# An attention and feed-forward kernel: one projection moved from block 2 to the end of block 1, and eight more filler matmuls in the opening

## Chip, cores, metric

One core of one Trainium2 chip. The metric is the device time of an execution in microseconds. Each run also has a profile, whose span (first to last instruction) is some 1.8 us shorter than the time of the same execution. TensorE is called PE, VectorE DVE, ScalarE ACT, GpSimd POOL, SyncE SP.

## The reference, cut to what matters

For each of 8 batches and 8 heads, K and V (1024 x 64) are projected along the sequence by E and F to 64 rows; q attends to these; the result, 8192 x 512, goes through a feed-forward layer with a quick GELU.

```python
k_proj = np.einsum('ks,bhsd->bhkd', E, k)
v_proj = np.einsum('ks,bhsd->bhkd', F, v)
scores = scale * np.matmul(q, k_proj.transpose(0, 1, 3, 2))
...                                   # softmax over the 64
x = np.matmul(attn, v_proj)           # to (8192, 512)
h = x @ w_in                          # 512 -> 2048
out = (h * (1.0 / (1.0 + np.exp(-1.702 * h)))) @ w_out
```

## The kernel before

It works in 16 blocks of 512 tokens, two to a batch. A block has 16 groups of four matmuls (ffn1, slots 0 to 15), then eight of eight (ffn2, slots O to O+7, with O = 16). Attention of later blocks is put into these slots: `at(j, slot, ...)` says behind which part of block j a piece comes. Each engine is given its work in the order of the program: in the profile DVE casts k_b of batch 2 at 100.95 us, behind the norm(3, 0) that stands ahead of it, though PE had ended that projection at 95.7. In norm(h, u) and scores(h, u), h counts blocks of 512 tokens (two to a batch) and u halves of the heads, so scores(4, 0) is the first attention of batch 2. The PSUM pools of the program have eight buffers in all, called banks here: four for f_ps, two for d_ps, two for n_ps.

```python
ps_f = ctx.enter_context(tc.tile_pool(name="ps_f", bufs=4, space=PSUM))
ps_d = ctx.enter_context(tc.tile_pool(name="ps_d", bufs=2, space=PSUM))
ps_n = ctx.enter_context(tc.tile_pool(name="ps_n", bufs=2, space=PSUM))

def load(b):                          # issued by POOL at the start of block 2(b-2)
    load_kv(k, kt, b, "k_sb")         # one buffer: waits for the projection of b-1
    if b == 1:
        load_kv(v, vt, b, "v_sb")
    load_q(b)                         # eight DMAs
    if b > 1:
        load_kv(v, vt, b, "v_sb")

def warm(n):                          # fillers: PE works on zeros, meant to keep its clock up
    w_ps = f_tile([P, TB])
    for _ in range(n):
        nc.tensor.matmul(w_ps, zeros[:, :P], zeros, start=True, stop=True)

def proj(b):                          # 16 matmuls, K and V in turn
    def go():
        kvps[b] = f_tile([P, H, D])
        for j in range(J):
            for e, r in enumerate((LO, HI)):
                nc.tensor.matmul(kvps[b][r], eft(j, slice(e * KP, (e + 1) * KP)),
                                 (kt, vt)[e][b][:, :, j, :], start=(j == 0), stop=(j == J - 1))
    return go

def kv_out(b):                        # DVE casts k_b, SP transposes it by DMA, DVE copies V
    ...
        nc.vector.tensor_copy(k_b, ps[LO])
        if b > 1:
            nc.sync.dma_start_transpose(out=kts[b % 2], in_=k_b.rearrange("k h d -> k (h d)"))
        v_out(b, ps)
...
at(1, O + 4, q_dma(2))                # SP transposes q of batch 2 by DMA
at(2, 1, norm(3, 0))                  # two reciprocals and two products on DVE
at(2, 2, proj(2), kv_out(2))
at(2, 11, norm(3, 1))
at(2, O, ...scores(4, 0)...)          # the first that needs kts of batch 2
```

The opening (the calls ahead of block 0) does the attention of the first tokens while K, Q, V, w_in and w_out arrive on one queue of POOL, in that order (later parts of Q come between V and w_in and among w_in); fillers stand where PE would wait.

The softmax here doesn't subtract the row's maximum and nothing guards it: scores larger than these inputs give would overflow.

## Time and profile before

| | |
|---|---|
| time, median of the 6 runs beside the change | 514.50 us (513.2 to 515.5) |
| execution that was profiled | 516.17 us, span 514.4 us, mean granted clock 0.996 |
| PE busy in that profile | 499.3 us |
| first K matmul, first ffn1, first ffn2 | 10.01, 23.46, 40.47 us |
| projection of batch 1, of batch 2, scores(4, 0) | 66.56, 93.81, 110.44 us |

### The profile page before, as it was taken

To read this page: it belongs to the slowest core of one execution; us is meant where nothing else is said; L and a number is where in the kernel's file an instruction comes from. 1 tells how busy PE (TensorE), PEld (TensorE's weight loads), DVE (VectorE), ACT (ScalarE), POOL (GpSimd) and SP (SyncE) were. 2 spreads that over 40 slices of the span, in tenths; PEclk is the share of its full clock that TensorE was granted. 3 is DMA by queue.
4 is the path that set the end of the run, shared out by engine and by line. 5 is a ranking of instruction groups with operands and counts; after the bars stand their busy time and mean duration, and the time that the engine had idled before them with its cause. 6 is when DMAs were issued, how large, how long until landed. Compare 5 with 4: busy or idle time off the path is not lost.

```text
span 514.4 us, 7185 instructions
## 1 busy us (share of the span) xinstructions
PE 499.3 (97%) x3040; PEld 232.0 (45%) x3090; DVE 171.6 (33%) x222; ACT 264.8 (51%) x444; POOL 78.0 (15%) x97
## 2 busy tenths in 40 slices
PE   6999999999999999999999999999999999999997
PEld 3585444434444444444444444444444444444444
DVE  4432214763871521416242251615214161511000
ACT  1576454554637446373655627375473737244351
POOL 6542051512400051000510023000000000000000
PEclk9999999999999999999999999999999999999999
DMA  9999999999999089670996339990602305050102
GB/s 157 197 202 207 190 152 171 214 157 134 210 118 240 1 142 215 129 178 6 223 179 181 76 80 217 121 246 1 169 1 59 107 3 163 1 165 1 82 1 82
DMA packets 124200, 66.58 MB, mean 129 GB/s; under 512 B 92252, under 2 KB 116060, under 8 KB 122248
## 3 DMA queue, kind: packets, MB, share of 16 engines
q0 software_dynamic: 84400, 29.37, 51.8%
q1 hardware_dynamic: 39688, 36.49, 28.2%
q8 instruction: 24, 0.39, 0.3%
q10 hardware_dynamic: 80, 0.26, 0.2%
q14 instruction: 8, 0.07, 0.0%
HBM read 70.78 MB, written 16.96 MB: 171 GB/s over the span
## 4 chain that ended last, share of the span: by engine, by line
PE 91%; DMA 3%; DVE 2%; issue 2%; ACT 1%; DVEq 0%; POOLq 0%
PE f_ps L401 42%; PE f_ps L369 40%; PE f_ps L166 2%; PE f_ps L263 2%; DMA kt<-k_b 2%; DMA k_sb<-in_k_dram 2%; DVE rdn L318 1%; PE n_ps L263 1%; PE f_ps L174 1%; PE n_ps L355 1%; PE d_ps L340 1%; PE d_ps L298 0%; PE f_ps L136 0%; PE f_ps L393 0%; DVE xT L319 0%
## 5 line engine op out<-in xcount | busy, mean ns | idle before, releaser
L369 PE MATMUL f_ps<-xT,w_in_sb 128*128 128x512 bf16 (+1 forms) x1071 | 225.4, 366 | 0.9
L401 PE MATMUL f_ps<-w_out_sb,gT 128*128 128x512 bf16 x976 | 221.5, 379 | 4.0 <-issue 3.5
L372 ACT ACTIVATE gT<-f_ps 128x512 bf16<-128x512 f32 (+1 forms) x270 | 152.1, 573 | 62.9 <-PE f_ps L369 61.7
L369 PEld LDWEIGHTS <-w_in_sb 128*128 128x128 bf16 x1088 | 105.5, 98 | 115.6 <-issue 2.1
L401 PEld LDWEIGHTS <-gT 128*128 128x128 bf16 x1008 | 95.5, 98 | 120.2 <-issue 11.3
L404 ACT COPY o_sb<-f_ps 128x512 f32<-128x512 f32 x63 | 36.9, 586 | 130.8 <-PE f_ps L401 121.0
L328 DVE TENSOR_TENSOR xT<-n_ps,rbc 128x512 bf16<-128x512 f32 x44 | 28.4, 686 | 203.3 <-PE n_ps L263 123.8
L301 DVE RECIPROCAL rden<-d_ps 128x512 f32<-128x512 f32 x22 | 72.2, 3322 | 0.0
L64 POOL DMA_DIRECT2D q_sb<-in_q_dram x56 | 49.1, 901 | 54.1 <-DMA k_sb<-in_k_dram 42.5
L279 ACT ACTIVATE expT<-f_ps 128x512 bf16<-128x512 f32 (+1 forms) x68 | 35.1, 571 | 27.8 <-PE f_ps L263 27.8
L58 POOL DMA_DIRECT2D k_sb<-in_k_dram x10 | 8.4, 845 | 175.6 <-PE f_ps L166 159.2
L318 DVE RECIPROCAL rdn<-d_ps 128x512 f32<-128x512 f32 x8 | 26.8, 3353 | 6.5 <-PE d_ps L263 6.5
L279 ACT ACT_TABLE_LOAD x13 | 16.7, 1283 | 5.8 <-PE f_ps L263 5.6
L220 DVE CAST k_b<-f_ps 64x512 bf16<-64x512 f32 x7 | 4.8, 682 | 44.2 <-PE f_ps L166 44.2
L283 ACT ACT_TABLE_LOAD x14 | 18.0, 1283 | 0.2
L166 PE MATMUL f_ps<-k_sb,eft 128*64 128x512 bf16 x56 | 13.4, 382 | 0.0
L166 PE MATMUL f_ps<-v_sb,eft 128*64 128x512 bf16 x56 | 13.4, 382 | 0.0
L395 DVE COPY o_sb<-f_ps 128x256 f32<-128x256 f32 x1 | 0.4, 425 | 38.6 <-issue 38.6
L263 PE MATMUL f_ps<-qT,kt 64*32 64x512 bf16 x240 | 12.3, 387 | 1.0 <-DMA kt<-k_b 1.0
L136 PE MATMUL f_ps<-zeros 128*128 128x512 bf16 x25 | 9.3, 484 | 1.6 <-DVE zeros L107 1.2
L263 PEld LDWEIGHTS <-kt 64*32 64x32 bf16 x272 | 4.0, 89 | 14.5 <-issue 12.9
L263 PE MATMUL n_ps<-expT,vq 64*32 64x512 bf16 x208 | 10.4, 377 | 0.0
(71 smaller groups left out, 132.7 us busy)
## 6 DMA issues: line engine op xcount, KB each, us to landing
out_dram<-o_sb SPq DMA_DIRECT2D x15, 1024.0 KB
rbc<-rdr SPq DMA_DIRECT2D x22, 512.0 KB
k_sb<-in_k_dram POOLq DMA_DIRECT2D x7, 1024.0 KB, 14.1
v_sb<-in_v_dram POOLq DMA_DIRECT2D x7, 1024.0 KB, 10.4
q_sb<-in_q_dram POOLq DMA_DIRECT2D x56, 128.0 KB, 14.0
w_in_sb<-in_moe_w_in_dram POOLq DMA_DIRECT2D x8, 256.0 KB, 11.7
w_out_sb<-in_moe_w_out_dram POOLq DMA_DIRECT2D x4, 512.0 KB, 14.8
out_dram<-o_sb SPq DMA_DIRECT2D x3, 256.0 KB
```

Of the source, the lines that this page charges most:

```text
L64: nc.gpsimd.dma_start(out=qt[b][:, j], in_=qv[:, j])
L166: nc.tensor.matmul(kvps[b][r], eft(j, slice(e * KP, (e + 1) * KP)), (kt, vt)[e][b][:, :, j, :], start=(j == 0), stop=(j == J - 1))
L263: nc.tensor.matmul(outs[i][r.start + c:r.start + c + 32], lhsTs[i][ri, c:c + 32], rhss[i][ri], start=True, stop=True)
L279: nc.scalar.activation(expT[h][:, 2 * u + i, ts], s_ps[i], AF.Exp, scale=scale)
L283: nc.scalar.preload_act_table(AF.Gelu_apprx_sigmoid)
L301: nc.vector.reciprocal(rden[:, e, :], d_ps[e])
L318: nc.vector.reciprocal(rd, d_ps[i])
L328: nc.vector.tensor_tensor(x_of(h)[:, 2 * u + i, :], n_ps[i], rbc[h][:, 2 * u + i, :], op=ALU.mult)
L369: nc.tensor.matmul(h_ps, w_in_sb[:, kc, fc * P:(fc + 1) * P], xT[j][:, kc, ts], start=(kc == 0), stop=(kc == KC - 1))
L372: nc.scalar.activation(gts[j][:, fc, ts], h_ps, AF.Gelu_apprx_sigmoid)
L401: nc.tensor.matmul(o_ps[n], gts[j][:, fc, n * P:(n + 1) * P], w_out_sb[:, fc, :], start=(fc == 0), stop=(fc == FC - 1))
L404: nc.scalar.copy(osb[j][:, n, :], o_ps.pop(n))
```

## The change

The intent: batch 2 gets projected before norm(3, 0) loads DVE, so that the transposed k_b is there when scores(4, 0) asks; and the fillers of the opening leave the four f_ps banks and fill more of the gaps, so that the clock of PE stays up.

```diff
--- before.py
+++ after.py
@@ -131,7 +131,7 @@
         return ps_f.tile(shape, dt, name="f_ps")
 
     def warm(n):
-        w_ps = f_tile([P, TB])
+        w_ps = ps_n.tile([P, TB], F32, name="n_ps")
         for _ in range(n):
             nc.tensor.matmul(w_ps, zeros[:, :P], zeros, start=True, stop=True)
 
@@ -150,7 +150,7 @@
     for i in range(2):
         nc.vector.tensor_copy(ffs[:, i * J // 2:(i + 1) * J // 2],
                               efts[i][:, :, None, KP:].to_broadcast([P, J // 2, 2, KP]))
-    warm(2)
+    warm(4)
 
     def eft(j, cols=slice(0, 2 * KP)):
         return efts[j // (J // 2)][:, j % (J // 2), cols]
@@ -179,7 +179,7 @@
         k_ps = proj0(0, h0, n)
         k_b = att.tile([KP, n, D], BF16, name=f"k0_b{h0}", bufs=1)
         nc.vector.tensor_copy(k_b, k_ps[LO])
-        warm(1)
+        warm(2)
         k_tr(0, k_b, h0 // 2)
 
     def k_tr(b, k_b, p0):
@@ -422,14 +422,15 @@
     warm(2)
     for u in range(2):
         scores(0, u, 0)()
+    warm(4)
+    v_piece(0, 4)
     warm(3)
-    v_piece(0, 4)
-    warm(2)
     for p in range(2):
         tok(0, p, 0)()
     v_piece(4, 2)
     warm(1)
     x_tr(0, 0, 0)()
+    warm(1)
     tok(0, 2, 0)()
     x_tr(0, 1, 0)()
     v_piece(6, 2)
@@ -471,7 +472,7 @@
         at(j, O + 5, gelu_table)
     at(1, O + 4, q_dma(2))
     at(2, 1, norm(3, 0))
-    at(2, 2, proj(2), kv_out(2))
+    at(1, O + 7, proj(2), kv_out(2))
     at(2, 11, norm(3, 1))
     at(2, O + 6, proj(3), kv_out(3), norm(4, 0))
     at(2, O, q_dma(3))
```

## The prediction

> **What bounds the kernel now.** I read the page first. Part 1 says that TensorE is busy for nearly the whole span, and part 2 that it runs at full clock in every slice:
>
> ```profile
> PE 499.3 (97%) x3040; PEld 232.0 (45%) x3090; DVE 171.6 (33%) x222; ACT 264.8 (51%) x444; POOL 78.0 (15%) x97
> PEclk9999999999999999999999999999999999999999
> ```
>
> So only idle time or slow clock of TensorE can be saved: 514.4 less 499.3 is 15.1 us of idle. The second view is the list of waits of PE alone, from 28 us to the end. It has two lines:
>
> ```profile
> PE f_ps L401 <- issue: 3.5, 22, 0.2
> PE f_ps L263 <- DMA kt<-k_b: 1.0, 1, 1.0
> ```
>
> The reader is to see that after 28 us one single wait is worth naming, 1.0 us, once. All else that a schedule can save lies in the first 28 us (15.1 less 4.5 makes 10.6 us of idle there, most of it before the first data arrive). The change goes for these two places.
>
> The third view is the chain that ended last, near that wait (start, length, what):
>
> ```profile
> 92.74 3.37 DVE rdn L318
> 96.20 0.69 DVE xT L319
> 96.89 3.27 DVE rdn L318
> 100.26 0.69 DVE xT L319
> 100.95 0.59 DVE k_b L220
> 101.57 8.82 DMA kt<-k_b
> 110.44 0.41 PE f_ps L263 x8
> ```
>
> Batch 2 is projected at 93.8 to 95.7, but VectorE takes the queue of two reciprocals and two products of norm(3, 0) first (8.1 us), casts k_b at 100.95, and the DMA transpose lands 8.82 us later, 1.0 us after PE wanted scores(4, 0).
>
> The fourth view is the timeline, of POOL and of PE, for what the earlier place of the projection needs:
>
> ```profile
> 80.98 0.87 POOL L58 DMA_DIRECT2D v_sb<-in_v_dram  x1 [0.33 <-issue]
> ...
> 88.74 1.89 PE L401 MATMUL f_ps<-w_out_sb,gT 128*128 128x512 bf16 x8
> 90.47 1.89 PE L369 MATMUL f_ps<-xT,w_in_sb 128*128 128x512 bf16 x8
> ```
>
> and the DMA view of 80 to 96 us:
>
> ```profile
> v_sb<-in_v_dram POOLq DMA_DIRECT2D x1, 1024.0 KB, 10.6
> ```
>
> V of batch 2 is issued at 80.98 and lands 10.6 us later, at 91.6. The new place of the projection is reached by PE at 90.6, when the last part of block 1 ends (the first row of block 2 starts at 90.47, and the chain has it take over at 90.63).
>
> The fifth view is busy time and clock in the opening, in stretches that I chose by the clock (PE, PEld, DVE, ACT, POOL, then PEclk, DMA share, GB/s):
>
> ```profile
> 11.67:15.08 3.41, 3.41 (x26) 2.12 (x27) 1.03 (x5) 0.00 (x0) 1.98 (x3) 0.51 1.31 204
> 8.26:11.67 3.41, 1.36 (x11) 0.92 (x11) 0.56 (x2) 0.00 (x0) 1.00 (x2) 0.99 1.42 195
> 4.85:8.26 3.41, 2.00 (x14) 0.85 (x12) 1.75 (x6) 1.20 (x2) 3.24 (x5) 1.00 1.15 156
> ```
>
> PE runs at half clock from 11.67 to 15.08, after a stretch in which it was busy for 1.36 of 3.41 us; the stretch before, with 2.00 of 3.41, was followed by full clock.
>
> [...] one half-speed stretch of 3.41 us, and one filler takes 0.63 us in it and 0.38 us outside. [...] these stretches put it between 40% and 59%, if the records' busy time is what counts. [...] The rows around the 1.0 us wait show no other matmul slipping in. [...] The program's pools take 4, 2 and 2, so the fillers get no new bank: they move from f_ps into the two of n_ps, which the x transposes use. No run so far shows what that costs.
>
> **The change, part by part.** *Projection.* Removed: the 1.0 us wait. The new order casts k_b before norm(3, 0), so at about 94 instead of 100.95. The transpose goes out behind the store of block 1 (issued at 93.28); even with 5 us for that store and 9 for itself it lands by about 108, and PE asks at 109.4 or later. I take the whole 1.0 us as removed. Added: PE reaches the projection at 90.63; its first V matmul cannot start before 91.6 plus the 0.13 us that the first K matmul of the kernel took after its landing, so 91.74. The first K half runs meanwhile beside nothing; the 8 pairs are then 8 x 0.215 = 1.72 and end at 93.46, against 90.63 + 1.85 = 92.48 without a wait. Cost: +1.0 us. The load of V hangs on the projection of batch 1 (its end lets K of batch 2 be issued, K's landing lets Q's last and V be issued), so this distance does not change when the opening shifts. Moved: 16 matmuls, no more and no fewer. Norm(3, 0) now comes after the projection, and norm(3, 1) follows it by 103.54 - 92.29 - 1.85 = 9.4 us of PE work where VectorE needs 0.4 + 8.1 = 8.5 us: just enough, no new wait. K of batch 3 is issued about 2 us earlier, which nothing waits for. Sum: -1.0 + 1.0 = 0.0 us, give or take 0.3.
>
> *Fillers.* Eight more 128x512 matmuls: 2 after the E/F transposes, 1 in each of three K pieces, 3 in the V part. The first two stand in the 2.29 us gap before K lands at 9.88 and cost nothing. They also cost nothing at full clock (0.215 us each) in gaps that PE has anyway. At half clock each takes 0.427, and in a K piece the gap is from the last projection matmul to the cast's end: 12.62 to 13.13. Two fillers (0.85) overrun it by 0.3 us, in two pieces: +0.6, of which about 0.2 is regained where fillers before the V piece no longer wait for the exponentials (0.26 idle at 16.57). Then x_tr(0, 1): with fillers between, all the x transposes fall into one bank of n_ps, so it waits for ScalarE's copy of x_tr(0, 0), from 20.59 to about 20.77: +0.2. So the opening costs +0.4 to +0.6 us if the clock still drops.
>
> If the fillers keep the clock up: the K pieces save 8 x 0.052 us twice (0.8), the fillers there and the transposes of Q some 0.4 more, until arrival of data limits it: Q's first part lands at 13.84 (issued 4.08), where PE began at 14.92, and V's first at 16.43, where PE began at 17.47. That is about 1.0 earlier, less 0.2 for x_tr: -0.8 us.
>
> Which? In the stretch 8.26 to 11.67 one filler more adds 0.21 us: 1.36 becomes 1.57, 46%. [...] I give staying at full clock 0.45. Mean of the opening: 0.45 x -0.8 + 0.55 x 0.5 = -0.1 us. From 28 us on PE has no slack in it, so what the opening gains or loses reaches the end.
>
> Sum: 514.3 + 0.0 - 0.1, and a little lower because the gain has the longer arm: **514.0 us**.
>
> **Rivals.** *A, V is there in time.* If the load landed before 90.6 (it would need 9.6 us; the loads of V in the trace take 10.1 at least), the wait is removed for nothing: -1.0 us, 513.2. For it speaks only that executions differ a little. *B, V comes late and k_b late too.* If the transpose behind the 1 MB store and the queue of Q's transpose landed after 110.4, both waits stand: +1.0, 515.2. Against it stands 14 us of room for a job of 8.8. *C, the clock stays up*: -0.8 and the middle even, 513.5; with A 512.4. *D, the clock drops as before and fillers lengthen the K pieces*: +0.5, 514.8. *E, VectorE becomes the bound in block 2*: the margin at norm(3, 1) is 0.9 us by my working; if kv_out pushed norm(3, 0) back by over that, some tenths of wait at L263 of d_ps come up.
>
> **Range and chances.** C and D alone span 513.5 to 514.8, the three times of before span 1.2 us[...], so a profile and a time can differ by some tenths. I take 512.9 to 515.0. 2% is 10.3 us, and all of PE's idle time is 15.1, most of it ahead of the first data: no rival comes near. Faster by over 2%: 0.01; within: 0.985; slower: 0.005.
>
> **What would show it.** In the profile after: no wait of L263 for kt<-k_b, and in its place one wait of PE at L166 (f_ps from v_sb) of about 1.0 us near 90.6; k_b cast near 94; the chain of waits naming v_sb. In the opening: 34 fillers into n_ps; the clock by stretches either whole after 5 us, with q_sb transposed near 14.0, or half for 3.4 us, with k_b transposes about 0.3 us behind their casts. A wait of x_tr (n_ps, L355) for ScalarE's copy near 20.7. No wait at all at L166 would prove the projection's sum wrong (rival A); a wait at L263 still there would prove B; an opening that ends over 1 us earlier or later than 23.46 (the first ffn1 matmul) would prove my opening wrong.

Cut from it, where marked, are general statements on the clock, the order of matmuls, the DMA engines and PSUM, which no trace of this case showed, and two clauses that rested on them. 514.3 + 0.0 - 0.1 comes to 514.2, and 514.0 was given. What the stretches "put between 40% and 59%" is the busy share at which the clock would turn, an estimate of mine from two stretches of the fifth view (1.36 us of 3.41 with half clock after it, 2.00 with full clock); the chance of 0.45 rests on it alone, the 46% with one filler more lying between the two, and a run refutes it below. That a matmul which waits holds up those behind it, on which the +1.0 us for V rests, I could read then only from the rows around the 1.0 us wait; in the changed kernel the first V matmul waited and all behind it came 0.7 us late.

## The result

The changed kernel took 514.45 us (514.05 to 515.34, 6 runs) against 514.50 us: ratio 1.0003, 95% interval 0.9987 to 1.002, the same. A ratio here is the mean time of one kernel's runs over that of the other's of the same rounds, so not quite the ratio of the medians quoted.

The profiles seem to say something else: span 512.6 against 514.4 us. First the waits of PE alone from 28 us on, of the changed kernel (total, times, longest):

```profile
PE f_ps L166 <- DMA v_sb<-in_v_dram: 0.3, 1, 0.3
PE f_ps L369 <- DMA w_in_sb<-in_moe_w_in_dram: 0.2, 1, 0.2
```

The wait for kt<-k_b is gone, and one for V stands in its place. The timeline of PE (start, length, what, [idle before]) shows what it really costs:

```profile
87.31 1.89 PE L401 MATMUL f_ps<-w_out_sb,gT 128*128 128x512 bf16 x8
89.13 0.40 PE L166 MATMUL f_ps<-k_sb,eft 128*64 128x512 bf16 x1
89.88 0.38 PE L166 MATMUL f_ps<-v_sb,eft 128*64 128x512 bf16 x1 [0.34 <-DMA v_sb<-in_v_dram]
89.88 0.40 PE L166 MATMUL f_ps<-k_sb,eft 128*64 128x512 bf16 x1
```

The first V matmul starts 0.75 us after the K matmul that it ought to go beside. The view of waits counts 0.34 us of it, since the K matmul's own record covers 0.40 us; the delay of all that follows is 0.7 us. The DMA view of 79 to 96 us has the same line for V as before (10.6 us from issue to landing), from an issue at 79.20: landing at 89.8. DVE (timeline) casts k_b ahead of norm(3, 0) now, as meant:

```profile
91.80 0.68 DVE L220 CAST k_b<-f_ps 64x512 bf16<-64x512 f32 x1 [3.91 <-PE f_ps L166]
92.51 0.87 DVE L214 CAST vq<-f_ps 64x256 bf16<-64x256 f32 x2
93.97 3.36 DVE L318 RECIPROCAL rdn<-d_ps 128x512 f32<-128x512 f32 x1 [0.59 <-PE d_ps L263]
```

In the opening, busy time and clock by stretches (PE, PEld, DVE, ACT, POOL, PEclk, DMA share, GB/s) show full clock where the first profile had half:

```profile
8.26:11.67 3.41, 3.19 (x31) 2.07 (x31) 1.12 (x4) 0.00 (x0) 1.92 (x3) 1.00 1.47 194
11.67:15.08 3.41, 3.41 (x47) 1.46 (x45) 0.90 (x3) 1.78 (x5) 1.05 (x2) 1.00 1.26 205
```

But the opening meets something that the first profile of before had not shown. The chain that ended last runs through two loads now, w_in in the opening and V in the middle:

```profile
16.54 11.49 DMA w_in_sb<-in_moe_w_in_dram
28.03 0.05 issue
28.07 2.81 PE f_ps L369 x24
...
79.20 10.63 DMA v_sb<-in_v_dram
89.83 0.04 issue
89.88 1.89 PE f_ps L166 x15
```

and the timeline of PE has the first of these waits:

```profile
28.07 1.16 PE L369 MATMUL f_ps<-xT,w_in_sb 128*128 128x256 bf16 x9 [0.21 <-DMA w_in_sb<-in_moe_w_in_dram]
```

PE can go on at 28.07 us only because the sixth piece of w_in landed at 28.03. The pieces before it hold PE up too, by less: the third, fourth and fifth land at 23.98, 25.32 and 26.66, and the first ffn1 group that needs each starts at 24.03, 25.36 and 26.71. So first ffn1 to first ffn2 takes 17.7 us here, and 17.0 in the first profile. In the chain of before, the same stretch belonged to PE's own work.

Cut at marks that both traces have, the difference of the two profiles is (differences of start times in the timelines, us; K means the first K matmul, P the first matmul of batch 1's projection):

| stretch | before | changed | difference |
|---|---|---|---|
| start to K | 10.01 | 8.40 | -1.61 |
| K to first ffn2 | 30.46 | 30.64 | +0.18 |
| first ffn2 to P | 26.09 | 26.09 | 0.00 |
| P to scores(4, 0) | 43.87 | 43.53 | -0.34 |
| scores(4, 0) to the end | 403.97 | 403.97 | 0.00 |

So 1.61 of the 1.77 us lie ahead of the first K matmul, which starts when K has landed (at 9.88 and 8.36 us); the change does not touch that load, issued at 1.25 us in both. That asks for more profiles of the kernel before, which the experiments bring.

One more thing that the table settles: the page of before lists 0.16 us of "issue" ahead of L401, 22 times, 3.5 us in all. In the changed kernel there is none, and yet the stretch that holds all 22 (scores(4, 0) to the end) is equally long. The pages say why: before has L401 x976, the changed kernel x1008, and both have 1008 weight loads of that line. Records of matmuls are missing, and a missing record looks like idle time.

### The profile page after: what moved, and what is told of

Read it like the earlier page. It is cut to its first block, busy times and chain, and to the rows that moved or that the text cites. A ratio compares the mean times of both kernels' runs of the same rounds, so it can differ in the third digit from the quotient of the medians.

```text
span 512.6 us, 7250 instructions
## 1 busy us (share of the span) xinstructions
PE 505.9 (99%) x3098; PEld 231.8 (45%) x3098; DVE 171.7 (33%) x222; ACT 264.8 (52%) x444; POOL 78.0 (15%) x97
## 4 chain that ended last, share of the span: by engine, by line
PE 82%; DMA 13%; issue 3%; POOL 1%; DVE 0%; ACT 0%; POOLq 0%
PE f_ps L369 38%; PE f_ps L401 38%; DMA v_sb<-in_v_dram 9%; DMA w_in_sb<-in_moe_w_in_dram 2%; PE f_ps L166 2%; DMA k_sb<-in_k_dram 2%; PE f_ps L263 2%; PE n_ps L263 1%; PE d_ps L298 0%; POOL k_sb L58 0%; PE f_ps L393 0%; POOL q_sb L64 0%; PE d_ps L263 0%; POOL q_sb L58 0%; POOL v_sb L58 0%
## 5 line engine op out<-in xcount | busy, mean ns | idle before, releaser
L401 PE MATMUL f_ps<-w_out_sb,gT 128*128 128x512 bf16 x1008 | 227.4, 379 | 0.0
L401 PEld LDWEIGHTS <-gT 128*128 128x128 bf16 x1008 | 95.6, 98 | 120.1 <-issue 11.3
L64 POOL DMA_DIRECT2D q_sb<-in_q_dram x56 | 49.1, 901 | 55.8 <-DMA k_sb<-in_k_dram 42.8
L136 PE MATMUL n_ps<-zeros 128*128 128x512 bf16 x34 | 11.5, 463 | 1.2 <-DVE zeros L107 1.2
L263 PE MATMUL n_ps<-expT,vq 64*32 64x512 bf16 x208 | 10.4, 377 | 0.0
## 6 DMA issues: line engine op xcount, KB each, us to landing
v_sb<-in_v_dram POOLq DMA_DIRECT2D x7, 1024.0 KB, 10.4
```

Of the source, the lines that this page charges most:

```text
L64: nc.gpsimd.dma_start(out=qt[b][:, j], in_=qv[:, j])
L263: nc.tensor.matmul(outs[i][r.start + c:r.start + c + 32], lhsTs[i][ri, c:c + 32], rhss[i][ri], start=True, stop=True)
L401: nc.tensor.matmul(o_ps[n], gts[j][:, fc, n * P:(n + 1) * P], w_out_sb[:, fc, :], start=(fc == 0), stop=(fc == FC - 1))
```

## The experiments

Twelve runs in three calls, five rounds each; every call timed the kernel before on the same chip (514.05, 514.01 and 514.35 us, 11 runs each). Theory 1 throughout: the two waits of the middle replace each other, and the opening is paced by arrival of data.

**b_again: the kernel before, unchanged.**

> The kernel before, unchanged, to learn how typical its one profile is: that execution took 516.17 us, its timed runs 513.2 to 515.5, and its first K landed at 9.88 us where the changed kernel's landed at 8.36. Theory 1 (the first profile was an outlier: late data and the half clock after it): the new profile has its first K near 8.4, a span of 512.3 to 513.3, and mean granted clocks of some runs at 0.999 or over. Theory 2 (before always loses 3.4 us at half clock): every run of it shows a clock near 0.996 to 0.997, the new profile too, and first ffn1 at about 22.5 to 23.5. In both: 514.5 us, the wait of 1.0 us for kt<-k_b stands.

513.38 us against 514.05 (ratio 0.9995, 0.9977 to 1.0012). Clock by stretches:

```profile
8.25:11.67 3.42, 2.96 (x30) 1.99 (x30) 1.12 (x4) 0.00 (x0) 2.16 (x3) 1.00 1.48 194
11.67:15.08 3.41, 2.99 (x44) 1.61 (x43) 0.90 (x3) 1.80 (x5) 0.95 (x3) 1.00 1.25 206
```

The first K landed at 8.12 us instead of 9.88, PE idled before it for 0.82 us instead of 2.29, and the clock stays full, with the old fillers. All six runs, and all 33 of the kernel before, have a mean clock of 0.999 or 1.000; the two profiles with one stretch of 3.41 us at half clock, the first and that of e_proj, have 0.996. So the half clock of the first profile belongs to one rare execution, in which K came late. That the idle time before K brought it about fits e_proj and e_none below, but no run repeats that execution, and in e_best PE stood idle for 1.83 us before K at full clock throughout. And that is the smaller surprise: its waits from 28 us on are only

```profile
PE f_ps L369 <- DMA w_in_sb<-in_moe_w_in_dram: 0.2, 1, 0.2
```

The 1.0 us for kt<-k_b, the target of the first part of the change, is not there (my expectation that it stands failed, and the span of 511.8 us lies below the 512.3 to 513.3 expected). From P, k_b's transpose was issued at +35.01 in both, but landed at +42.90 here and at +43.83 in the first profile; PE asks at +42.88. It is a race that ends by chance between 0 and 1 us late.

**e_proj: only the projection moved.**

```diff
-    at(2, 2, proj(2), kv_out(2))
+    at(1, O + 7, proj(2), kv_out(2))
```

> Only the projection of batch 2 moved, the fillers as before. Theory 1 (the wait for the transposed k_b is replaced by one for V): no wait for kt<-k_b, 0.5 to 1.0 us lost at the first V matmul of batch 2 instead; the time changes by -0.5 to 0.0 us against before. Rival (the projection costs or gains a whole microsecond and the fillers do the opposite): -1.0 or +1.0.

514.32 us (ratio 1.0019, 0.9997 to 1.0042): the median is 0.3 us above before, where -0.5 to 0.0 had been expected. The wait for kt<-k_b is gone. The profiled execution, 517.22 us, shows how bad the new wait can be:

```profile
91.05 0.38 PE L166 MATMUL f_ps<-v_sb,eft 128*64 128x512 bf16 x1 [2.68 <-DMA v_sb<-in_v_dram]
```

V landed at +27.04 from P, 3.0 us after PE stood there. In the stretch with this wait PE was busy for 0.79 of 3.41 us, and in the next 3.41 us the clock was 0.50 (windows):

```profile
88.43:91.84 3.41, 0.79 (x8) 0.56 (x9) 0.00 (x0) 0.23 (x1) 0.00 (x0) 1.00 0.86 118
91.84:95.25 3.41, 3.41 (x15) 1.24 (x10) 1.28 (x3) 0.00 (x0) 0.92 (x2) 0.50 1.25 365
```

scores(4, 0) came at +47.50, 4.7 us after the +42.8 of an execution with no wait: some 3.0 for V and, by my estimate, some 1.7 (half of the 3.41 us at a clock of 0.50) for the clock. The other five runs took 513.99 to 514.83. Why V was so late the trace does not settle. P came 1.2 us earlier than in the changed kernel's profile (63.97 against 65.13 us), and V landed 1.2 us later (91.01 against 89.83), though both were issued at 79.2. One of the sixteen parts of the last Q load of batch 1 landed at 64.30 us, 5.0 us after the other fifteen (all sixteen by 60.69 in the changed kernel's profile). K of batch 2, issued at 66.19, then took 11.6 us to land instead of 10.4; whether the one led to the other was not tested. So V's arrival did not follow PE here: PE was 1.2 us ahead, and waited 3.0 us instead of 0.7.

**e_fill: only the fillers changed.**

```diff
-    at(1, O + 7, proj(2), kv_out(2))     # against the changed kernel
+    at(2, 2, proj(2), kv_out(2))
```

> Only the fillers changed (count and bank), the projection where it was. Theory 1 (opening paced by the arrival of w_in): the clock is full from some 6 us on, the first ffn1 comes up to 1 us earlier than before, but PE waits for w_in near 28 us, and the end of the opening (first ffn2) moves by under 0.4 us; time within 0.4 us of before; the wait for kt<-k_b of 1.0 us stands. Rival (the fillers are worth their clock): -0.8 us or more. Rival (fillers lengthen the opening): +0.4.

514.53 us (ratio 1.0019, 0.9998 to 1.004): nothing gained. As theory 1 said: full clock from 4 us, a wait for w_in at 27.60, K to first ffn2 30.26 us (b_again 30.59), and the wait for kt<-k_b stands, 0.75 us. The median is 0.5 us above before, just outside theory 1's 0.4 and near the last rival's +0.4; but the opening of the profile is not longer, so that rival's mechanism is not seen.

**e_late: as the changed kernel, the projection one ffn1 group later.**

```diff
-    at(1, O + 7, proj(2), kv_out(2))
+    at(2, 0, proj(2), kv_out(2))
```

> As the changed kernel, but batch 2 is projected one ffn1 group later, at the first slot of block 2, still ahead of norm(3, 0) on VectorE. Theory 1 (the new wait is V's arrival, 0.5 to 0.7 us short): the wait at the first V matmul falls to 0 to 0.2 us, no wait for kt<-k_b, time -0.3 to -0.6 against the changed kernel. Rival (what was lost in block 2 is not the arrival of V): as the changed kernel.

513.83 us (ratio to before 1.0004, 0.9984 to 1.0023). In the trace the mechanism is plain: PE reaches the place at +24.86 from P, V has landed at +24.86, and neither wait is left:

```profile
89.70 0.40 PE L166 MATMUL f_ps<-k_sb,eft 128*64 128x512 bf16 x1
89.74 0.38 PE L166 MATMUL f_ps<-v_sb,eft 128*64 128x512 bf16 x1
```

scores(4, 0) at +42.82, 0.7 us ahead of the changed kernel. Its median is 0.6 us under the 514.45 of the changed kernel, which was not timed beside it, and 0.2 us under the kernel before: by the times alone it is not told from either.

**a_again: the changed kernel once more.**

> The changed kernel once more, beside the next three on one chip. Theory 1 (V of batch 2 lands at a time set by the DMA stream, 24.7 us or more after PE starts the projection of batch 1; PE is at the new place after 24.0): a loss of 0.6 us or more at the first V matmul, no wait for kt<-k_b, scores(4, 0) 43.5 us or more after the projection of batch 1 (before: 42.9 to 43.9). Time 514.4, within 0.2% of before. Rival (the wait of the one profile was chance): no wait, scores(4, 0) at +42.9.

514.74 us against 514.01: ratio 1.0018, interval 1.0003 to 1.0033: slower by 0.2%, clear of 1. V landed at +24.73, its first matmul at +24.77, scores(4, 0) at +43.56: the loss of 0.7 us is there again.

**e_best: fillers of before, the projection at the first slot of block 2.** (Against before: `at(2, 2, proj(2), kv_out(2))` becomes `at(2, 0, ...)`.)

> The kernel before with its fillers, and batch 2 projected at the first slot of block 2, ahead of norm(3, 0). Theory 1: neither wait (V is asked for at +24.9 after the projection of batch 1, where it had landed at +24.7 to +25.1; k_b is cast near +26.9), so scores(4, 0) at +42.8 to +43.2; time 0.3 to 0.6 us under before and under the changed kernel. Rival (the wait of 1.0 us in the first profile of before is rare, so there is nothing to gain): as before.

513.50 us (ratio 1.0002, 0.9983 to 1.0021; one run of 515.73). No wait, scores(4, 0) at +42.81. The median is 0.5 us lower, the mean is not: two of six runs had a clock of 0.997 and took 514.53 and 515.73.

**e_vfirst: the changed kernel with V of batch 2 loaded ahead of its Q.**

```diff
-        if b == 1:
+        if b <= 2:
             load_kv(v, vt, b, "v_sb")
         load_q(b)
-        if b > 1:
+        if b > 2:
```

> The changed kernel, with V of batch 2 loaded ahead of its Q (as batch 1 has it), so that V lands some 7 us earlier. Theory 1 (the wait at the new place is for V): no wait at the first V matmul, proj(2) runs at +24.0 without a gap. But Q lands about 5 us later, its transposes and the store and transpose behind them on the same queue start 5 us later, and kt lands at +43 to +45, where PE asks at +42.8: a wait for kt<-k_b of 0 to 2 us may come back. Rival (the wait at L166 is not V's arrival): it stays.

513.50 us (513.18 to 513.85; ratio 0.999, 0.9977 to 1.0002). V lands at +17.38 and the wait is gone: K's and V's first matmul both start at +24.00. The fear for the transposes was half right: k_b's now lands at +41.65, 1.2 us ahead of PE. So it was V's arrival that held the projection at its new place. The times say so too: on the same chip, the changed kernel (a_again) took 514.31 to 515.96 us, so no run of one overlaps the other. The medians lie 1.24 us apart, of which the profiles put 0.75 between P and scores(4, 0) (43.56 against 42.81).

**e_none: the changed kernel without fillers after the first twelve.**

```diff
     def warm(n):
+        if n < 12:
+            return
```

> The changed kernel without any filler after the first twelve. Theory 1 (fillers keep the clock up, though the added ones were not needed for it): PE falls to half clock for at least one stretch of 3.4 us between 8 and 20 us, the first ffn1 comes 0.5 to 1.5 us later than in the changed kernel (21.4), and part of that is hidden behind the arrival of w_in: time +0.3 to +1.5 us. Rival (the opening is paced by data alone): full clock or not, first ffn2 within 0.2 us, time as the changed kernel.

515.81 us (ratio 1.0043, 1.0023 to 1.0063): the fillers are worth something. Windows:

```profile
5.42:8.83 3.41, 1.37 (x12) 0.83 (x11) 1.88 (x4) 1.20 (x2) 2.62 (x4) 1.00 1.18 182
8.83:12.24 3.41, 2.90 (x18) 1.86 (x17) 0.64 (x2) 0.00 (x0) 2.12 (x3) 0.50 1.48 193
12.24:15.66 3.42, 2.27 (x44) 1.51 (x43) 1.37 (x5) 0.95 (x3) 0.92 (x3) 1.00 1.24 205
15.66:19.07 3.41, 2.82 (x18) 2.12 (x19) 0.94 (x3) 0.85 (x4) 2.30 (x3) 0.50 1.55 190
```

Two stretches at half clock; first ffn1 14.2 us after K (13.0 in the changed kernel), first ffn2 31.30 (30.64). Not all of the loss is the opening's: of the 2.0 us between the spans of this profile and the changed kernel's, 0.4 lie ahead of K, 0.7 between K and first ffn2, and 0.9 between P and scores(4, 0), where V landed at +25.63. All six runs have clocks of 0.987 to 0.997. So fillers are needed, and those of before were already enough in its usual executions.

**e_vbest, e_vbank, e_vcount, e_vboth: the fillers taken apart.** All four have the projection at the end of block 1 and V first, so the middle has no wait. Fillers: 26 in f_ps (as before); 26 in n_ps; 34 in f_ps; 34 in n_ps (e_vfirst again).

> Fillers as before (f_ps, 26 of them), batch 2 projected at the end of block 1, V of batch 2 loaded ahead of its Q. Theory 1 (no wait of either kind, fillers of before suffice when the first K lands near 8.4): full clock, no wait at the projection, scores(4, 0) at +42.8 after the projection of batch 1, time as e_vboth within 0.3 us, 0.4 to 0.7 us under before. Rival (the added fillers carry the gain of 0.5 us that the V-first kernel showed): as before.

> As e_vbest, but the 26 fillers write to the n_ps banks. Theory 1 (the bank matters for a few tenths of waiting at most, of which 0.26 us at the third filler group): the filler ahead of the first V piece no longer waits for the exponentials; first ffn1 at most 0.3 us earlier, time within 0.3 us of e_vbest. Rival (transposes of x wait in the shared banks): first ffn1 0.2 us later after the first K matmul.

> As e_vbest, but with the 34 fillers, in f_ps as before. Theory 1 (fillers at full clock fit the gaps): first ffn1 within 0.2 us of e_vbest counted from the first K matmul, time within 0.3 us. Rival (more fillers lengthen the opening): 0.3 to 0.6 us later.

> The same kernel as e_vfirst, repeated beside the three above: 34 fillers in n_ps. Theory 1: 513.5 us within 0.3, no wait at the projection nor for kt. Rival (the 0.1% under before was chance): as before.

| | fillers | time, us | ratio to before (514.35) | K to first ffn1 | K to first ffn2 | wait for w_in near 27.5 |
|---|---|---|---|---|---|---|
| e_vbest | 26, f_ps | 513.59 (513.08 to 515.7) | 0.9996, 0.9976 to 1.0017 | 12.70 | 30.39 | 0.22 |
| e_vbank | 26, n_ps | 513.66 (513.16 to 514.26) | 0.9992, 0.9975 to 1.001 | 12.89 | 30.54 | 0.21 |
| e_vcount | 34, f_ps | 513.53 (512.77 to 514.06) | 0.9986, 0.997 to 1.0002 | 12.70 | 30.39 | 0.23 |
| e_vboth | 34, n_ps | 513.24 (512.71 to 513.64) | 0.998, 0.9965 to 0.9996 | 12.57 | 29.77 | none |

The four medians lie within 0.42 us and the intervals overlap: neither the bank nor the count is shown to matter. Theory 1's expectation for the time holds to 0.05 us (e_vbest lies 0.35 above e_vboth, and 0.3 was the limit). The first ffn1 of e_vbank came 0.19 us later than that of e_vbest, as its rival had said, but that of e_vboth, with the same bank, 0.13 earlier: one profile of each does not settle it.

What separates the openings is whether PE meets the sixth piece of w_in before it has landed. Of the twelve experiments' profiles, three had an opening without that wait and without half clock (e_proj, e_best, e_vboth); there the first ffn2 comes 29.49, 29.51 and 29.77 us after K. The eight others at full clock have 30.13 to 30.59. With the old fillers (26, f_ps) it was two of four, with the new ones (34, n_ps) one of five: chance, as far as this can tell. The landing marks (a load lands in sixteen parts, and the packed trace has a time for each) show what PE waits for: in the nine profiles with this wait, the changed kernel's own included, the last part of the sixth piece of w_in landed 0.5 to 1.2 us after the fifteenth; in the first profile, e_proj, e_best and e_vboth it was 0.03 to 0.2 us. The lag starts with the second load of Q, whose last part lands near 20 us. Why one part falls behind is not shown.

e_vbest and e_vcount also show a late V of batch 3 (0.6 us more from scores(4, 0) to the end than the 403.97 of the others), two of the five profiles with V of batch 2 loaded first; whether that order made it late was not tested.

e_vfirst and e_vboth are the same kernel: 12 runs, 513.50 us in the first six and 513.24 in the second, none above 513.85. It is the only version whose interval lies below 1, 0.2% under before and only in the second (one of twelve comparisons, so no strong proof), and the steadiest. Above 1 lie a_again and e_none.

## Why the prediction was right, step by step

The number 514.0 for 514.45, inside the range, and "within 2%" were right. That it came so close is in part luck: a forecast of no change (514.3) would have been closer, both waits of the middle were taken too large and cancelled, and the -0.1 for the opening was the mean of two branches of which neither came. The steps fared unequally.

- **Projection, wait removed: right, but mis-sized as a fixed cost.** I took "the whole 1.0 us as removed". Three executions with the old place had 0.99, 0.06 and 0.75 us. The transpose lands between +42.90 and +43.83 from P, and PE asks at +42.88; one profile had caught its bad end.
- **Projection, wait added: mechanism right, size 1.0 for a measured 0.7.** V landed at +24.70 and +24.73 in the two profiles of the changed kernel (I took the +25.05 of the first profile) and PE stands there at +24.0. Over all profiles with V last, V came between +24.70 and +27.04: never in time, so rival A was not seen in any of the nine, and the distance from P, which I took as fixed, is not. e_late and e_vfirst, which give V 0.86 us and 7.3 us more room, lose the wait.
- **Sum of the middle, 0.0 +- 0.3: near zero, but the margin was too narrow.** P to scores(4, 0): 43.53 and 43.56 after, 43.87 and 42.94 before; 42.81 with no wait. So the change gains 0.3 us against the first profile of before and loses 0.6 against the second.
- **norm(3, 1), E: right.** No wait at d_ps appears; the second norm follows the first at its 9.3 us (93.53 to 102.82).
- **Rival B did not occur**: kt landed at +38.78 and +37.85, 4.7 us and more ahead of PE.
- **Fillers: the premise failed.** "If the clock still drops" and the chances 0.45 and 0.55 treated the half clock of the first profile as a property of the kernel. It was a property of one execution in which K came 1.8 us late; b_again ran at full clock with the old fillers.
- **The turning point "between 40% and 59%", my estimate from two stretches, is refuted** as a share of recorded busy time: in e_none a stretch with 66% (2.27 of 3.42 us, two thirds of it transposes and small score matmuls) was followed by half clock (0.50) too.
- **"-0.8 us if the fillers keep the clock up": wrong.** I carried the gain to the end of the opening by the arrival of Q and V alone and left out w_in. K to first ffn1 was 12.96 us, 0.5 less than the 13.45 of before, but to the first ffn2 it was 30.64 against 30.46: the sixth piece of w_in landed at 28.03 (28.49 in the first profile), PE waited for it, and the gain was gone. I had the landing times in the trace and did not follow that queue past V.
- **x_tr(0, 1), +0.2: wrong.** In the changed kernel (timeline) it does not wait for the copy, which ends at 18.22:

```profile
17.85 0.37 ACT L357 COPY xT<-n_ps 128x256 bf16<-128x256 bf16 x1
17.96 0.27 PE L340 MATMUL f_ps<-vx,expT 128*128 128x130 bf16 x2
...
18.09 0.28 PE L355 MATMUL n_ps<-ident,x_sb 128*128 128x128 bf16 x2
```

  It follows tok by 0.13 us, as before (0.12). My count of whose turn each bank is was not what was built; how it was built I did not look up.
- **"15.1 us of idle": overstated** by the missing records told above, 3.5 us of them past 28 us.
- **Smaller slips.** "Full clock in every slice" reads too much into the page: a 9 stands for 90% or more of a slice of 12.9 us, and the half clock of 11.67 to 15.08 hides in two of them, as the fifth view shows. The sum 514.3 + 0.0 - 0.1 is 514.2, and the step to 514.0 has no working; C with A is 512.5.

What stays open: why one of the sixteen parts of each load falls behind from about 19 us on in some executions (in the changed kernel the marks of one load lie 1.0 us apart for V and 2.0 us for the Q after it; 1.2 for both in e_proj), and whether the added fillers make slow executions rarer. Clocks of 0.997 or less came in e_best and e_vbest (old fillers) in 4 of 12 runs, in e_fill in 1 of 6, in e_vfirst and e_vboth in none of 12; but in none of the 39 timed runs of the kernel before that have a clock on record either (the first profile's execution, 0.996, comes on top).

## What to carry to other kernels

Before moving work ahead of a wait, write down when each of its inputs lands from the same mark on the same clock: here the new place came 0.7 us before V, and one slot later, or the load reordered, was free. Take a second profile of the kernel before as soon as the first belongs to an execution outside the timed range: both things that this change set out to mend were, in good part, accidents of one execution. And follow a gain in the opening to the last transfer that the opening needs, not to the first ones.

## What was measured and stays unexplained

- The clock. Stretches of 3.41 us with 23% (e_proj), 40% (first profile, e_none) and 66% (e_none) of recorded busy time were followed by half clock, one with 59% (first profile) was not. No busy share sorts these, and what decides the clock is not shown.
- Missing matmul records showed up as idle time: 976 of 1008 records of one line, 22 gaps of 0.16 us, 3.5 us in all, in an execution that lost nothing there. The traces of e_vbest, e_vbank, e_vcount and e_vboth have the same 976, with 21 gaps.
- The small DMA transpose of k_b (64 x 512 bf16) beside loads took, from issue to landing, 7.9, 8.6 and 8.8 us in the old place of the program and 7.9 to 12.1 us in the new ones. The spread in the old place is what made the wait for it come and go.
